# First MLP pipelined one tile deeper on VectorE and PE, recurrence operations bound behind the tile they are issued in, reciprocals of K in the second MLP

## The chip, the cores and the metric

The kernel runs on one core of a Trainium2 chip. The time is the device time of one execution in microseconds. The engines are called PE (TensorE, matrix products), DVE (VectorE), ACT (ScalarE), POOL (GpSimd) and SP (SyncE, which issues the DMAs). PE reads its left operand in a weight load (PEld) that overlaps the matmul before it.

## The reference

The reference is a gated linear recurrence over 768 steps for 32 heads, whose output goes through two MLPs. Cut to what matters:

```python
# recurrence, per batch and head (D = 48): a = a_re + i a_im, |a| clipped to 0.999
for t in range(S):
    S_re, S_im = ar * S_re - ai * S_im + k_t v_t^T, ar * S_im + ai * S_re
    y[t] = q_t @ S_re
# first MLP (384 -> 2048 -> 384)
h = x @ w_in
P = a[0] + a[1]*h + a[2]*h**2 + a[3]*h**3
Q = 1.0 + abs(b[0])*abs(h) + abs(b[1])*h**2
x = (P / (Q + 1e-06)) @ w_out
# second MLP (384 -> 1536 -> 384)
g = x @ w_gate
return (g * sigmoid(g) * (x @ w_val)) @ w_out2
```

All of it is float32. A product at float32 accuracy is made of products of a high and a low part (hi, lo) of each operand, three of the four.

## The kernel before

**Stages.** The 3072 tokens are worked off in six pairs of units, 512 tokens to a pair, numbered 0 to 5. The startup makes the recurrence inputs and attention of pair 0 and converts the first weights. Then each pair runs the first MLP (16 tiles of 128 hidden columns) and the second MLP (12 tiles), both in `moe`. PE's accumulators `acc` collect the output over the tiles of an MLP.

**A tile of the first MLP.** PE makes `ph` in nine up matmuls (L179 to L181). ACT makes `w` = |b1 ph| (L211) and `u` (L212, a scale and a bias). DVE forms numerator and denominator in three operations (L218 into `w`, L221 and L223 into `u`). ACT takes |w| (L222), then Ln and Exp into `r` (called at L223 to L225 of the code, recorded at L117, the line of the helper `fact`). The inner function `divide` puts on DVE `hi` (L228), `w` (L229) and `u` (L230), and on POOL `lo` (L231); it also queues the tile's nine down matmuls in `pend`, six with `hi` (L186, L187) and three with `lo` (L190). `flush` issues what is queued. `u` and `w` have three buffers each, `hi`, `lo` and `r` two. `HALF` is 1: in the iteration of tile f the code first flushes the down matmuls of tile f-2, then calls `divide` of tile f-1, then writes the three forming operations of tile f; an order dependence puts the first of them behind the last operation of `divide`.

**Between the MLPs** the output is split into `x1h` (ACT, L122) and `x1l` (DVE, L123).

**A tile of the second MLP.** PE makes `pg` and `pv` in 18 up matmuls; ACT takes silu of `pg` into `u` (L117); DVE multiplies by `pv` (`w`, called z in the code, L261); ACT rounds it to `hi` (L262); DVE makes `lo` (L265); nine down matmuls follow one tile later. The outputs are copied by ACT (L271) and stored.

**Work woven in.** While pair i runs, `tick`, called once in each tile, issues work of later pairs. First the recurrence's elementwise work of pair p = i + 1 and later: 36 steps a pair (`EW`): seeds, a scan of the complex gates, the products of Q (L531), and nine steps for K: squares (L566, L567), their reciprocals by Ln and Exp (recorded at L117 as `t`), two operations (L588, L589), and for each unit a scaling (L592) and products (L531). `ENDS` gives for each pair how far (in pairs) these steps are to be when its first and second MLP end, `SPAN` in how many tiles of the first MLP its share is issued. Second, the 17 attention steps of pair i + 1 on PE, ACT and DVE (`kT`, `pp`, `pm`, `S`, `py`, `xl`; L619 to L652); `AT` gives the tiles in which they are issued, `HOLD` how many are kept for the gap between the MLPs.

**Order.** The code is issued in program order; a scheduler then fills each engine's queue by priority, with its own estimates of when operands are ready, and so pulls operations that depend on nothing late ahead of those that do. On the chip each engine runs its queue in order. Ln and Exp share one table on ACT, silu has another; a switch is an ACT_TABLE_LOAD (L104). `order(later, earlier)` adds a dependence that fixes the order of two instructions.

In pair 0 weights are also converted from their stored form (`raw`, L129 to L141, on DVE and ACT) as they are first needed, and written back for the later pairs.

## Time and profile before

| | before |
|---|---|
| median of 3 runs | 1451.88 us (1448.75 to 1460.53) |
| the profiled execution | 1443.08 us |
| its span, first to last instruction | 1441.2 us |
| mean granted TensorE clock (1 = 2.4 GHz, 0.5 = 1.2 GHz) | 0.919 |
| PE busy | 1149.0 us (80%) |
| DVE busy | 987.0 us (68%) |
| ACT busy | 699.1 us (49%) |
| POOL busy | 127.3 us (9%) |
| chain of work that ended last, by engine | PE 50%, DVE 21%, ACT 17%, POOL 5%, DMA 4% |

The shares of busy time are averages over stages with different limits, so the table alone doesn't say what bounds the kernel: the stages do. PE's matmuls are pipelined and their ends are modelled, so PE's busy time also holds short waits. The profile names an instruction by its line, its engine, what it writes and what it reads (buffer numbers left out). An entry in brackets is the idle time of the engine just ahead of the instruction, with what ended it. "L12" is line 12 of the kernel.

### The profile page before, as it was taken

The page shows a single profiled execution, that of the slowest core. Times are in us where ns is not written, and L with a number is a line of the kernel's source. Part 1 is how long each engine was busy: PE and PEld are TensorE (multiplying, and loading weights), DVE is VectorE, ACT ScalarE, POOL GpSimd, SP SyncE. Part 2 cuts the span into 40 slices and gives each one's busy share as a digit, 9 for nine tenths or more (in the row PEclk, how much of TensorE's full clock was granted, in tenths as well). Part 3 has the DMA queues.
Part 4 walks back from the last instruction along what each step waited for, and adds up shares of the span by engine and source line. Part 5 has one row for each costly group of instructions (what it writes and reads, how often), then busy time and mean ns, then how long its engine had stood idle before and what let it go on. Part 6 is the DMA issues. An engine that isn't in the chain of part 4 may idle for free.

```text
span 1441.2 us, 15114 instructions
## 1 busy us (share of the span) xinstructions
PE 1149.0 (80%) x5314; PEld 916.1 (64%) x5314; DVE 987.0 (68%) x1601; ACT 699.1 (49%) x1081; POOL 127.3 (9%) x110
## 2 busy tenths in 40 slices
...
GB/s 227 110 232 206 175 252 246 191 187 224 204 248 245 250 138 130 231 239 227 115 112 136 282 225 161 115 100 201 274 195 146 116 151 195 180 109 131 132 175 47
DMA packets 128291, 261.51 MB, mean 181 GB/s; under 512 B 8016, under 2 KB 85072, under 8 KB 127440
## 3 DMA queue, kind: packets, MB, share of 16 engines
...
HBM read 210.11 MB, written 50.33 MB: 181 GB/s over the span
## 4 chain that ended last, share of the span: by engine, by line
PE 50%; DVE 21%; ACT 17%; POOL 5%; DMA 4%; issue 3%; POOLq 0%; SPq 0%; ACTq 0%; DVEq 0%
ACT r L117 5%; POOL lo L231 5%; PE acc L190 5%; PE acc L186 5%; PE acc L187 4%; PE pg L179 4%; PE pg L180 4%; PE pg L181 4%; PE pv L179 3%; PE pv L180 3%; PE pv L181 3%; PE py L646 3%; DVE hi L228 3%; DVE u L230 3%; ACT u L212 3%
## 5 line engine op out<-in xcount | busy, mean ns | idle before, releaser
L186 PE MATMUL acc<-hi,wt 128*128 128x512 f32 x504 | 220.6, 438 | 69.0 <-DVE hi L228 68.8
L231 POOL TENSOR_TENSOR lo<-u,r 128x512 fp32r<-128x512 f32 x96 | 126.6, 1319 | 1229.8 <-DVE u L230 1088.1
L187 PE MATMUL acc<-hi,wt 128*128 128x512 f32 x504 | 212.3, 421 | 0.0
L190 PE MATMUL acc<-lo,wt 128*128 128x512 f32 x504 | 159.2, 425 | 59.4 <-POOL lo L231 58.9
L261 DVE TENSOR_TENSOR w<-pv,u 128x512 f32<-128x512 f32 x72 | 49.8, 691 | 190.8 <-PE pv L181 190.7
L186 PEld LDWEIGHTS acc<-hi,wt 128*128 128x128 f32 x504 | 102.5, 203 | 114.6 <-DVE hi L228 93.2
L179 PE MATMUL ph<-xh,wt 128*128 128x512 f32 x288 | 124.4, 432 | 49.0 <-ACT wt L138 35.7
L190 PEld LDWEIGHTS acc<-lo,wt 128*128 128x128 f32 x504 | 93.0, 198 | 105.6 <-POOL lo L231 90.8
L211 ACT ACTIVATE w<-ph,par 128x512 f32<-128x512 f32 x96 | 65.9, 686 | 157.5 <-DVE u L230 132.5
L228 DVE SCALAR_TENSOR_TENSOR hi<-u,par,r 128x512 fp32r<-128x512 f32 x96 | 71.9, 749 | 92.9 <-ACT r L117 92.4
L181 PE MATMUL ph<-xh,wt 128*128 128x512 f32 x288 | 119.0, 413 | 2.9 <-DVE wt L141 2.9
L180 PE MATMUL ph<-xl,wt 128*128 128x512 f32 x288 | 118.8, 412 | 0.0
L117 ACT ACTIVATE u<-pg 128x512 f32<-128x512 f32 x72 | 43.0, 598 | 154.9 <-PE pg L181 154.9
L187 PEld LDWEIGHTS acc<-hi,wt 128*128 128x128 f32 x504 | 103.1, 205 | 19.5
L262 ACT ACTIVATE hi<-w 128x512 fp32r<-128x512 f32 x72 | 45.4, 630 | 124.8 <-DVE w L261 124.5
L179 PEld LDWEIGHTS ph<-xh,wt 128*128 128x128 f32 x288 | 58.2, 202 | 72.6 <-ACT wt L138 38.9
L619 PE MATMUL pk<-ident,st 96*128 96x96 f32 x160 | 23.8, 275 | 92.5 <-DMA st<-qs 91.8
L212 ACT ACTIVATE u<-ph,par 128x512 f32<-128x512 f32 x96 | 74.7, 778 | 40.7 <-POOL lo L231 40.5
L179 PE MATMUL pg<-x1h,wt 128*128 128x512 f32 x216 | 89.0, 412 | 1.1 <-ACT x1h L122 1.1
L180 PE MATMUL pg<-x1l,wt 128*128 128x512 f32 x216 | 86.7, 401 | 0.0
L181 PE MATMUL pg<-x1h,wt 128*128 128x512 f32 x216 | 86.4, 400 | 0.0
L179 PE MATMUL pv<-x1h,wt 128*128 128x512 f32 x216 | 85.0, 393 | 0.0
(110 smaller groups left out, 2513.0 us busy)
## 6 DMA issues: line engine op xcount, KB each, us to landing
...
```

Of the source, the lines that this page charges most:

```text
L117: i = act(*args, **kw)
L179: t_.matmul(ph, whi, xh[:, k, :], start=(k == 0), stop=False)
L180: t_.matmul(ph, whi, xl[:, k, :], start=False, stop=False)
L181: t_.matmul(ph, wlo, xh[:, k, :], start=False, stop=(k == KT - 1))
L186: t_.matmul(acc[m], wt[:, 0, c : c + 128], hi, start=st, stop=False)
L187: t_.matmul(acc[m], wt[:, 1, c : c + 128], hi, start=False, stop=False)
L190: t_.matmul(acc[m], wt[:, 0, c : c + 128], lo, start=False, stop=sp)
L211: act(w, ph, AF.Abs, scale=b1)
L212: act(u, ph, AF.Identity, scale=a3, bias=a2)
L228: stt(hi, u, a0, r, ADD, MUL)
L231: g_.tensor_tensor(lo, u, r, MUL)
L261: tt(z, pv, sg, MUL)
```

## The change

Three things change. First, in the first MLP `divide` of tile f-1 is called after the forming operations of tile f and after that tile's `tick`, its first operation is ordered behind the last forming operation of tile f, and the forming operations of tile f are ordered behind the last operation of the `divide` before. `flush(gf)` keeps one tile's down matmuls pending, so they are issued one tile later. `hi` and `lo` are allocated in `divide`. Second, DVE operations issued by `tick` through `tt` and `stt` get an order dependence: they stay behind the tile's last forming operation (first MLP) or behind its `z` (second MLP). All operations through `tt` and `stt` are then recorded at L87, the line of the wrapper. Third, the tables `ENDS`, `SPAN` and `AT` change: pair 1's to pair 3's second MLPs now finish a pair's 36 steps, K's reciprocals among them, where before eight steps were left for the next pair's first MLP, and the attention steps of pairs 2 to 5 begin at tile 1 instead of tile 4 (pair 1: 12 instead of 10).

```diff
@@ -48,9 +48,9 @@
 EARLY1 = range(7, 16)
 CV = (5, 4)
 EW = 36
-ENDS = ((1.06, 1.5), (2.06, 2.8), (3.06, 3.8), (4.06, 4.8), (5.0, 5.0), (5.0, 5.0))
-SPAN = (16, 10, 5, 5, 5, 5)
-AT = ((16, 16, 0, 11), (10, 16, 0, 6), (4, 16, 0, 1), (4, 16, 0, 1), (4, 16, 0, 1), (4, 16, 0, 1))
+ENDS = ((1.06, 1.5), (2.06, 3.0), (3.06, 4.0), (4.06, 5.0), (5.0, 5.0), (5.0, 5.0))
+SPAN = (16, 11, 8, 8, 5, 5)
+AT = ((16, 16, 0, 11), (12, 16, 0, 6), (1, 16, 0, 1), (1, 16, 0, 1), (1, 16, 0, 1), (1, 16, 0, 1))
 HOLD = (0, 3, 4, 4, 4, 0)
 XMAX = 1e18
 NTINY = 1e-30
@@ -77,7 +77,21 @@
 ):
     nc = tc.nc
     v_, s_, g_, t_ = nc.vector, nc.scalar, nc.gpsimd, nc.tensor
-    tt, stt, act = v_.tensor_tensor, v_.scalar_tensor_tensor, s_.activation
+    act = s_.activation
+    pin = {"on": False, "at": None}
+
+    def held_back(op):
+        def f(*args, **kw):
+            i = op(*args, **kw)
+            if pin["on"] and pin["at"] is not None:
+                order(i, pin["at"])
+            return i
+
+        return f
+
+    tt, stt = held_back(v_.tensor_tensor), held_back(v_.scalar_tensor_tensor)
     MUL, ADD, SUB, MIN, MAX = ALU.mult, ALU.add, ALU.subtract, ALU.min, ALU.max
 
     dram = ctx.enter_context(tc.tile_pool(name="dram", bufs=1, space=DRAM))
@@ -192,7 +206,7 @@
         def mt(tag, dt=F32):
             return mp.tile([128, gf, T], dt, tag=tag, name=tag, bufs=M_BUFS.get(tag, 3))
 
-        pend, half = [], []
+        pend, half, divided = [], [], []
 
         def flush(n):
             while len(pend) > n:
@@ -207,38 +221,36 @@
                 wts.append(wt)
                 up(ph[:, j, :], wt, 0, x_hi, x_lo)
             u, w, r = (mt(n) for n in ("u", "w", "r"))
-            hi, lo = mt("hi", F32R), mt("lo", F32R)
             act(w, ph, AF.Abs, scale=b1)
             act(u, ph, AF.Identity, scale=a3, bias=a2)
-            if len(half) > HALF - 1:
-                flush(0)
-                last = half.pop(0)()
-            else:
-                last = None
             p = stt(w, w, b0, ph, ADD, MUL)
-            if last is not None:
-                order(p, last)
+            if divided:
+                order(p, divided[-1])
             tt(u, u, ph, MUL)
             act(w, w, AF.Abs)
-            stt(u, u, a1, ph, ADD, MUL)
+            formed = stt(u, u, a1, ph, ADD, MUL)
             fact(r, w, AF.Ln, bias=cst[:, 2:3])
             fact(r, r, AF.Exp, scale=-1.0)
 
-            def divide(f=f, wts=wts, u=u, w=w, r=r, hi=hi, lo=lo):
-                stt(hi, u, a0, r, ADD, MUL)
+            def divide(f=f, wts=wts, u=u, w=w, r=r):
+                hi, lo = mt("hi", F32R), mt("lo", F32R)
+                first = stt(hi, u, a0, r, ADD, MUL)
                 stt(w, w, 1.0 + EPS, hi.bitcast(F32), ADD, MUL)
-                last = stt(u, u, a0, w, ADD, SUB)
+                divided.append(stt(u, u, a0, w, ADD, SUB))
                 g_.tensor_tensor(lo, u, r, MUL)
                 for j in range(gf):
                     pend.append((acc, wts[j], DM, hi[:, j, :], lo[:, j, :], f + j == 0, f + j == F1 - 1))
-                return last
+                return first
 
             half.append(divide)
-            tick(0)
+            tick(0, formed)
+            if len(half) > HALF:
+                flush(gf)
+                order(half.pop(0)(), formed)
         while half:
-            flush(0)
+            flush(gf)
             half.pop(0)()
-        tick(2)
+        tick(2, None)
         flush(0)
         xh = xp.tile([128, KT, T], F32R, tag="xh", name="x1h")
         xl = xp.tile([128, KT, T], F32R, tag="xl", name="x1l")
@@ -258,10 +270,10 @@
             sg, z = mt("u"), mt("w")
             hi, lo = mt("hi", F32R), mt("lo", F32R)
             fact(sg, pg, AF.Silu)
-            tt(z, pv, sg, MUL)
+            formed = tt(z, pv, sg, MUL)
             act(hi, z, AF.Copy)
             flush(0)
-            tick(1)
+            tick(1, formed)
             tt(lo, z, hi.bitcast(F32), SUB)
             for j in range(gf):
                 pend.append((acc2, wts[j], 0, hi[:, j, :], lo[:, j, :], f + j == 0, f + j == F2 - 1))
@@ -415,7 +427,7 @@
                         t_.transpose(px[:, m, :], rows[:, m * 128 : (m + 1) * 128], ident)
                     cs = slice(n * CH, (n + 1) * CH)
                     split(px, xh[:, :, cs], xl[:, :, cs])
-                moe(pools, 512, xh, xl, out[:, :, bass.ds(j * (UPB * 512) + k * 512, 512)], lambda ph: None, silu, feed(stored, pools[3]))
+                moe(pools, 512, xh, xl, out[:, :, bass.ds(j * (UPB * 512) + k * 512, 512)], lambda ph, ins: None, silu, feed(stored, pools[3]))
 
     with ExitStack() as es:
         ps = es.enter_context(tc.tile_pool(name="ps", bufs=5, space=PSUM))
@@ -749,10 +761,11 @@
                     next(at, None)
 
 
-            def tick(ph, cnt=[0, 0], eb=eb, e0=e0, e1=e1, n=n, at=at, at_to=at_to, at_n=at_n, w=AT[i], i=i):
+            def tick(ph, ins, cnt=[0, 0], eb=eb, e0=e0, e1=e1, n=n, at=at, at_to=at_to, at_n=at_n, w=AT[i], i=i):
                 if ph == 2:
                     at_to(at_done[0] + HOLD[i])
                     return
+                pin["on"], pin["at"] = True, ins
                 cnt[ph] += 1
                 t = cnt[ph]
                 lo, hi = ((eb, e0), (e0, e1))[ph]
@@ -764,6 +777,7 @@
                 if ph == 1 and t == n[1]:
                     ew_to(EW * (i + 1))
                     run(at)
+                pin["on"] = False
 
             if i:
                 lnexp()
```

What this does to the queues is shown at three places, from the lists of each engine's instructions in order. Numbers behind a name tell the buffers apart.

The first place is DVE in the first MLP of the last pair. `ph` is the output of the up matmuls; an operation that reads it belongs to the forming of a tile, one that writes or reads `hi` or reads `r` to the division. Before:

```order
L218 SCALAR_TENSOR_TENSOR w_8959<-w_8959,par_90,ph_8946 128x512
L221 TENSOR_TENSOR u_8958<-u_8958,ph_8946 128x512
L223 SCALAR_TENSOR_TENSOR u_8958<-u_8958,par_90,ph_8946 128x512
L228 SCALAR_TENSOR_TENSOR hi_8961<-u_8958,par_90,r_8960 128x512
L229 SCALAR_TENSOR_TENSOR w_8959<-w_8959,hi_8961 128x512
L230 SCALAR_TENSOR_TENSOR u_8958<-u_8958,par_90,w_8959 128x512
L218 SCALAR_TENSOR_TENSOR w_8997<-w_8997,par_90,ph_8984 128x512
L221 TENSOR_TENSOR u_8996<-u_8996,ph_8984 128x512
```

After, the same operations at L87:

```order
L87 SCALAR_TENSOR_TENSOR w_8916<-w_8916,par_90,ph_8903 128x512
L87 TENSOR_TENSOR u_8915<-u_8915,ph_8903 128x512
L87 SCALAR_TENSOR_TENSOR u_8915<-u_8915,par_90,ph_8903 128x512
L87 SCALAR_TENSOR_TENSOR hi_8935<-u_8877,par_90,r_8879 128x512
L87 SCALAR_TENSOR_TENSOR w_8878<-w_8878,hi_8935 128x512
L87 SCALAR_TENSOR_TENSOR u_8877<-u_8877,par_90,w_8878 128x512
L87 SCALAR_TENSOR_TENSOR w_8954<-w_8954,par_90,ph_8941 128x512
L87 TENSOR_TENSOR u_8953<-u_8953,ph_8941 128x512
L87 SCALAR_TENSOR_TENSOR u_8953<-u_8953,par_90,ph_8941 128x512
```

Before, a tile's division (`hi`, `w`, `u`) follows the forming of the same tile. Now the division of `u_8877` stands behind the forming of `u_8915`, the next tile.

The second place is DVE in the second MLP of pair 2: the tiles 2 to 4 of 12. `pv` is the value product of the second MLP; `qp` are the products of Q, `t6` squares of K. Before:

```order
L261 TENSOR_TENSOR w_5273<-pv_5249,u_5272 128x512
L531 TENSOR_TENSOR qp_5700<-q_5698,a_4421 128x8x6x16
L265 TENSOR_TENSOR lo_5275<-w_5273,hi_5274 128x512
L531 TENSOR_TENSOR qp_5700<-q_5698,a_4421 128x8x6x16
L531 TENSOR_TENSOR qp_5744<-q_5742,a_4421 128x8x6x16 x2
L567 TENSOR_TENSOR t6_5751<-t6_5751 128x8x96
L261 TENSOR_TENSOR w_5318<-pv_5294,u_5317 128x512
L567 TENSOR_TENSOR t6_5808<-t6_5808 128x8x96
L265 TENSOR_TENSOR lo_5320<-w_5318,hi_5319 128x512
L261 TENSOR_TENSOR w_5369<-pv_5345,u_5368 128x512
L265 TENSOR_TENSOR lo_5371<-w_5369,hi_5370 128x512
L261 TENSOR_TENSOR w_5416<-pv_5392,u_5415 128x512
```

After (`t3`, `a` and `T2` are the recurrence's scan):

```order
L87 TENSOR_TENSOR w_5277<-pv_5253,u_5276 128x512
L87 SCALAR_TENSOR_TENSOR t2_5244<-t1_4583,t2_5244 128x4x192
L87 TENSOR_TENSOR t3_5294<-a_4366 128x768
L87 TENSOR_TENSOR a_4366<-a_4366,t2_5244 128x1536
L87 TENSOR_TENSOR a_4366<-t3_5294 128x192 x2
L87 TENSOR_TENSOR lo_5279<-w_5277,hi_5278 128x512
L87 TENSOR_TENSOR t3_5294<-a_4366 128x768
L87 TENSOR_TENSOR w_5327<-pv_5303,u_5326 128x512
L87 TENSOR_TENSOR a_4366<-t3_5294 128x192 x2
L87 TENSOR_TENSOR t3_5294<-a_4366 128x768
L87 TENSOR_TENSOR lo_5329<-w_5327,hi_5328 128x512
L87 TENSOR_TENSOR a_4366<-t3_5294 128x192 x2
```

Before, the tiles' `w` and `lo` have at most three recurrence operations between them, and from the fourth tile on none; now scan operations of the next pair stand behind each `w`, some ahead of `lo` and some behind it.

The third place is ACT near the end of the same second MLP; `u` from `pg` is silu, `hi` the rounded product, `t6` K's squares and their Ln and Exp. After:

```order
L131 ACTIVATE u_5661<-pg_5637 128x512
L578 ACTIVATE t6_5679<-a_4366 128x1536
L578 ACTIVATE t6_5684<-a_4366 128x1536
L118 ACT_TABLE_LOAD
L274 ACTIVATE hi_5663<-w_5662 128x512
L131 ACTIVATE t6_5679<-t6_5679,cst_91 128x8x96
L131 ACTIVATE t6_5684<-t6_5684,cst_91 128x8x96
L131 ACTIVATE t6_5679<-t6_5679 128x8x96
L131 ACTIVATE t6_5684<-t6_5684 128x8x96
L118 ACT_TABLE_LOAD
L131 ACTIVATE u_5714<-pg_5694 128x512
L274 ACTIVATE hi_5716<-w_5715 128x512
```

Before, no table load stood between two tiles of a second MLP: the load and the Ln and Exp of K stood behind its last silu. Now K's squares, a load, the Ln and Exp and a load back stand between the silus of tiles 9 and 10 (counted from 0), and a third load stands behind the last silu for the next pair's first MLP.

## Rows read from the trace of the kernel before

**Rows 1.** Windows by stage: length, busy time per engine (instructions), PEclk, DMA share, GB/s.

```profile
0.00:168.50 168.50, 48.36 (x277) 45.61 (x277) 134.00 (x241) 75.12 (x107) 0.71 (x14) 0.85 0.57 189
168.50:308.40 139.90, 91.54 (x278) 60.87 (x279) 127.34 (x178) 100.51 (x152) 24.05 (x16) 0.77 0.66 222
308.40:427.00 118.60, 118.60 (x638) 101.92 (x638) 97.67 (x187) 68.15 (x123) 0.00 (x0) 0.90 0.62 211
427.00:557.70 130.70, 99.11 (x441) 74.81 (x439) 107.90 (x171) 77.06 (x116) 20.47 (x16) 0.91 0.63 205
557.70:644.60 86.90, 86.68 (x425) 72.44 (x424) 44.16 (x80) 26.90 (x42) 0.00 (x0) 1.00 0.70 214
644.60:777.60 133.00, 110.92 (x544) 89.20 (x542) 106.40 (x189) 75.18 (x120) 20.52 (x16) 0.90 0.46 148
777.60:854.60 77.00, 76.79 (x339) 62.98 (x338) 38.11 (x50) 24.93 (x37) 0.00 (x0) 1.00 0.77 236
854.60:982.90 128.30, 109.74 (x576) 88.43 (x575) 107.41 (x191) 74.81 (x117) 20.50 (x16) 0.92 0.43 139
982.90:1060.00 77.10, 76.88 (x339) 62.99 (x339) 39.64 (x57) 25.19 (x37) 0.00 (x0) 1.00 0.77 240
1060.00:1175.80 115.80, 100.94 (x528) 81.21 (x527) 79.55 (x116) 59.25 (x93) 20.53 (x16) 0.96 0.45 145
...
1252.60:1358.60 106.00, 78.58 (x279) 51.48 (x278) 67.26 (x96) 54.80 (x83) 20.52 (x16) 0.95 0.36 122
```

**Rows 2.** Timeline, first MLP of the last pair: start, duration, instruction [idle before, releaser].

```profile
1291.81 0.75 DVE L228 SCALAR_TENSOR_TENSOR hi<-u,par,r 128x512 fp32r<-128x512 f32 x1 [2.19 <-ACT r L117]
...
1293.33 0.75 DVE L230 SCALAR_TENSOR_TENSOR u<-u,par,w 128x512 f32<-128x512 f32 x1
...
1294.25 1.29 POOL L231 TENSOR_TENSOR lo<-u,r 128x512 fp32r<-128x512 f32 x1 [5.22 <-DVE u L230]
...
1295.57 0.78 ACT L212 ACTIVATE u<-ph,par 128x512 f32<-128x512 f32 x1 [0.71 <-POOL lo L231]
...
1296.24 0.62 ACT L222 ACTIVATE w<-w 128x512 f32<-128x512 f32 x1
...
1297.65 0.63 ACT L117 ACTIVATE r<-r 128x512 f32<-128x512 f32 x1
...
1298.32 0.75 DVE L228 SCALAR_TENSOR_TENSOR hi<-u,par,r 128x512 fp32r<-128x512 f32 x1 [2.20 <-ACT r L117]
```

**Rows 3.** Waits in the last pair's first MLP: total us, times, longest.

```profile
DVE hi L228 <- ACT r L117: 33.3, 16, 3.1
```

**Rows 4.** Timeline of ACT in the second MLP of pair 3.

```profile
1011.60 0.63 ACT L262 ACTIVATE hi<-w 128x512 fp32r<-128x512 f32 x1 [2.24 <-DVE w L261]
...
1017.72 0.63 ACT L262 ACTIVATE hi<-w 128x512 fp32r<-128x512 f32 x1 [2.24 <-DVE w L261]
```

**Rows 5.** Timeline of DVE in the first MLP of pair 3.

```profile
890.67 0.74 DVE L228 SCALAR_TENSOR_TENSOR hi<-u,par,r 128x512 fp32r<-128x512 f32 x1
...
895.32 1.89 DVE L469 TENSOR_TENSOR a<-a,t 128x1536 f32<-128x1536 f32 x1
...
898.66 0.74 DVE L228 SCALAR_TENSOR_TENSOR hi<-u,par,r 128x512 fp32r<-128x512 f32 x1
```

**Rows 6.** Groups by line, DVE, first and last of the recurrence's 36.

```profile
L437 DVE TENSOR_TENSOR t<-a 128x768 f32<-128x768 f32 x42 | 40.7, 969 | 0.4
...
L491 DVE MEMSET E<- 128x6 f32 x2 | 0.1, 63 | 0.0
```

**Rows 7.** Timeline of PE in the first MLP of pair 3, an attention step.

```profile
882.10 1.08 PE L623 MATMUL pp<-st 96*128 96x128 f32 x8
```

**Rows 8.** ACT, end of pair 1's second MLP (timeline), and its squares (by line).

```profile
636.76 1.28 ACT L104 ACT_TABLE_LOAD   x1
638.05 1.77 ACT L117 ACTIVATE t<-t,cst 128x768 f32<-128x768 f32 x2
...
L566 ACT ACTIVATE t<-a 128x1536 f32<-128x1536 f32 x12 | 17.5, 1478 | 0.2 <-DVE a L521 0.2
```

## The prediction

> **What bounds the kernel now.** I read the busy times by stage first [rows 1]: one window per MLP, cut where the first MLP's first ScalarE operation and the second MLP's first x1h start. In the last pair no attention and no recurrence work is left, and its first MLP still takes 106.0 us, with PE busy 78.6, DVE 67.3 and ACT 54.8: no engine is full. The timeline inside it shows why [rows 2]. From one `hi` to the next pass 6.51 us (1291.81 to 1298.32): DVE makes `hi`, `w`, `u` of tile k; GpSimd can then make `lo` (1294.25, 1.29 us); only when `lo` has released its `u` buffer does ACT write the `u` of a later tile (1295.57); behind that in ACT's queue stand |w|, Ln and Exp of tile k+1 (1296.24 to 1298.28); then DVE makes the next `hi`, after 2.20 us of idling. The waits of this stage say the same in sum: DVE waited 33.3 us for ACT's `r` in 16 tiles [rows 3]. It is a ring of dependences, run through once per tile. PE needs 18 matmuls a tile. In the second MLP, where PE never waits, ScalarE's `hi` comes every 6.12 us [rows 4] for 27 matmuls, 0.227 us each, so 18 are 4.1 us. DVE's six operations a tile are 67.3 us in 96 instructions [rows 1], 4.2 a tile; with small gaps I take 4.36.
>
> In pairs 1 to 3 the first MLP takes 130.7, 133.0 and 128.3 us [rows 1]. There recurrence work of a later pair stands between `hi`, `w` and `u`: one tile of pair 3 went from 890.67 to 898.66, 8.0 us, with a 1.89 us recurrence product inside it [rows 5]. The second MLPs of pairs 2 and 3 meanwhile have DVE busy for 38.1 and 39.6 of 77 us while PE is full at granted clock 1.00 [rows 1]: DVE is idle where PE is the bound, and loaded where the ring is.
>
> **The change, part by part.** *The ring.* In the new order (the first place shown) DVE forms tile k+1 before it divides tile k, and PE's down matmuls come one tile later. The ring then spans two tiles: 6.5/2 = 3.3 us a tile, and what is left is DVE's 4.36 and PE's 4.1. The `u` buffer that ACT waits for comes free by the same `lo`, now with a tile of DVE work to spare. Last pair: 106.0 less 15 steps of 6.51 leaves 8.4 us for filling and draining; 15 steps of 4.36, that 8.4, and 1.5 because the last two tiles' divisions now interleave make 75, so **-31**. If DVE and PE, so nearly equal, jostle at 4.7 a tile, it is -26.
>
> *The recurrence work in the first MLPs.* One pair's recurrence costs DVE 61.6 us: 36 groups of lines 162 to 168 and 437 to 592, from 40.7 us down, sum to 369.6 over six pairs [rows 6]. I priced each DVE row of both orders with the mean duration of its group. The first MLP's queue goes in pair 1 from 121.6 to 103.8 us, pair 2 from 123.3 to 81.8, pair 3 from 122.6 to 83.1, pair 4 from 84.2 to 79.8. PE has there 16 x 4.1 = 66 plus attention: 273 small matmuls a pair at about 0.1 us (eight took 1.08 [rows 7]), 13 of the 17 attention steps, so some 18 us: 84 in all. With 13 us more, the 8.4 of filling and draining and some 5 for waits of attention steps, I get 97 for pairs 2 to 4 against 133.0, 128.3 and 115.8: **-36, -31, -19**. Pair 1 is DVE's 103.8 plus 8: 112, **-19**. Attention could take back more: kT's copy stands in ACT's queue behind a `u` that waits for `lo`, so PE's attention matmuls can wait for `lo` and two ACT operations (1.29 + 0.78 + 0.62 = 2.7 us [rows 2]) four times a pair. The bounds are 0 and 11 us a pair; I take the 5, and keep the other 6 in each of three pairs, +18, for the range.
>
> *The second MLPs.* They take over what the first ones lose (the second place shown): pair 1's DVE queue goes from 41.8 to 78.9 us, pair 2's from 33.1 to 74.5, pair 3's from 36.0 to 75.5, against PE's 12 x 6.12 = 73.4. By tile pair 2 reads 4.8, 7.0, 6.8, 6.5, 6.9, 9.2, 6.0, 5.6, 5.9, 3.3, 6.2, 6.2: where DVE is above 6.1 it sets the step, in sum +6. That a tile costs the larger of the two and not their sum is shown by pair 0's second MLP: 97.7 us of DVE beside 118.6 of always busy PE at clock 0.90 [rows 1]; one after the other they would need over 73 + 98 = 171.
>
> *K's reciprocals* (the third place shown). Between two silus ACT now runs two squares, a table load, two Ln, two Exp and a second load. Before, the load and the Ln were at the end of the second MLP: load 1.28, two Ln 1.77, a square 1.48 [rows 8]. With two Exp taken as the Ln, the block is 2.96 + 1.28 + 1.77 + 1.77 + 1.28 = 9.1 us in a tile of 6.1; silu comes 3 us late, but its `down` stands behind the next tile's up matmuls (4.1 us). Bounds 0 and 3 a pair; I take 2.4. Second MLPs: **+3, +8.5, +7.5** (pair 1's was longer, 86.9, and absorbs more).
>
> The Trainium skill (page "ScalarE: Activation LUTs", section "What ACT_TABLE_LOAD costs") says that a switch costs 1283 ns for the load and about 1380 ns of drain. The trace has the first number exactly, but the first Ln started 1.29 us after the load did [rows 8], so no drain shows here. By the page the six added loads would cost up to 6 x 1.38 = 8 us more, by the row nothing.
>
> *Pair 0.* 43.6 us of pair 1's recurrence work used to run in the startup, where DVE was busy 134.0 of 168.5 us [rows 1]; bound behind a tile it moves into pair 0's first MLP, whose DVE queue goes from 141.7 to 167.5, and that stage already lasts as long as its queue (139.9, DVE 127.3 busy). That is +26. Against it the first conversions of weights find a freer DVE and the first up matmuls start about 10 us earlier by my walk through the order: **+16**, bounds 0 (the startup gives all of it back) and +26. Second MLP: 111.5 to 112.9, **+2**.
>
> Sum: +16 +2 -19 +3 -36 +8.5 -31 +7.5 -19 +0 -31 +0 = **-99 us**, made against the profiled execution of 1443.08 (span 1441.2): 1344. The median of the runs, 1451.88, lies 8.8 above it; with that the forecast is **1353 us**.
>
> **Rivals.** (a) *The pins cost much more.* DVE runs in order, and an operation bound behind a tile waits in line with everything behind it. In pair 0 conversions wait for their loads, and if those waits are no longer filled the stage costs +26 twice; that is +36 on top of the +16; with attention's +18 the gain is halved: -45, about 1407. For it: pair 0 has PEclk 0.77 [rows 1], the level of 1.2 GHz for some 46% of the stage, and PE waits there often. Against: pairs 4 and 5, with fewer recurrence rows, keep 0.95 and 0.96.
>
> (b) *The ring does not open*, because ACT still issues the waiting `u` ahead of |w|. Then the first MLPs keep their 6.5 us a tile; pairs 2 and 3 gain only what the moved work cost them above it (16 x 6.51 + 13 = 117: -16 and -11), and with the +37 of costs it ends at 1443 + 37 - 27 = 1453, by the median 1462. Against: the order puts a whole tile of DVE work between the `lo` and the first reader of that `u`.
>
> (c) *Slower.* Work bound behind `z` also stands ahead of `lo` of the same tile, and PE's down matmuls need `lo`. If PE could do nothing meanwhile, each second MLP of pairs 1 to 3 would take the 77 us of PE's pace and its 57 us of recurrence work one after the other, 134: +47, +57 and +57. With pair 0's +18 that is +179 against gains of 136: 1486 by the profiled run, 1495 by the median. It decides once 0.73 of that work is uncovered. Against: pair 0's second MLP [rows 1], where it is covered; the next tile's 18 up matmuls stand ahead of the waiting `down`.
>
> (d) *More than forecast*: the startup gives back all that pair 0 takes (+16 becomes 0), and attention fits into the tiles, so that pairs 2 to 4 need 84 + 8.4 = 92 instead of 97 (-15): 1322. For it: DVE was busy 0.8 of the startup. Against: PE and DVE then both have to run full.
>
> **Chances.** Forecast 0.60 (own range 1328 to 1380), (a) 0.20, (d) 0.08, (b) 0.05, (c) 0.07. The time is the forecast's. The range leaves out (b), (c), the part of (a) above 1412 and the far end of (d), together 0.2: 1315 to 1412. About 1% is what a measurement of this kernel can tell from no change: faster by more 0.87, within it 0.06 ((b) and a tail of (a)), slower 0.07 ((c)).
>
> **What would show it.** Ring right: `hi` to `hi` near 4.4 us in the last pair and no DVE wait for `r` of over 1 us; wrong: still 6.5. Moved work right: first MLPs of pairs 2 and 3 below 100 us, second ones at 84 to 86; (c) would show second MLPs above 110 with PE waiting for `lo`. Pair 0 right: its first MLP near 156; (a) would show it above 170, or PEclk below 0.85 in pairs 2 to 4. Reciprocals right: 18 loads of 1.28 us, the tile behind them late by under 3.5 us. The forecast is wrong if the second MLPs and pair 0 together give back over 80 us.

## The result and the profile after

The changed kernel takes 1341.18 us, the median of 4 runs (1337.3 to 1343.35), against 1455.05 (1448.75 to 1460.53, 4 runs) beside it: a ratio of 0.9216, 95% interval 0.9168 to 0.9263. The forecast was 1353 with a range of 1315 to 1412, and faster. The profiled execution has a span of 1339.4 us and a mean clock of 0.923; the sum of the forecast's terms, -99 us, meets -101.8 between the two spans.

| | after |
|---|---|
| span | 1339.4 us |
| PE busy | 1106.4 us (83%) |
| DVE busy | 984.0 us (73%) |
| ACT busy | 701.4 us (52%) |
| chain of work that ended last | PE 67%, DVE 16%, ACT 7%, POOL 1% |

The work is the same but for six more table loads on ACT; the chain moved to PE. These are the windows by stage, cut like [rows 1] (startup, then first and second MLP of each pair; columns: length, busy time of PE, weight loads, DVE, ACT and POOL with the number of instructions, PEclk, DMA share, GB/s):

```profile
0.00:156.80 156.80, 47.82 (x277) 45.62 (x277) 97.82 (x159) 61.92 (x89) 0.72 (x14) 0.88 0.60 203
156.80:321.40 164.60, 98.30 (x278) 65.30 (x279) 152.48 (x243) 105.04 (x157) 24.68 (x16) 0.72 0.53 174
321.40:434.60 113.20, 109.71 (x637) 93.43 (x636) 95.56 (x180) 74.40 (x134) 0.00 (x0) 1.00 0.73 251
434.60:545.20 110.60, 85.00 (x385) 66.21 (x385) 97.11 (x145) 75.27 (x112) 20.84 (x16) 0.92 0.70 225
545.20:638.90 93.70, 93.47 (x485) 78.84 (x485) 73.42 (x133) 33.28 (x48) 0.00 (x0) 1.00 0.61 198
638.90:739.60 100.70, 96.80 (x540) 83.90 (x539) 75.01 (x111) 70.41 (x118) 20.91 (x16) 0.93 0.62 201
739.60:817.70 78.10, 77.88 (x343) 63.45 (x342) 69.44 (x126) 30.82 (x43) 0.00 (x0) 1.00 0.70 226
817.70:929.20 111.50, 107.60 (x573) 94.02 (x571) 76.01 (x114) 70.78 (x116) 20.87 (x16) 0.86 0.54 167
929.20:1005.70 76.50, 76.26 (x336) 62.25 (x335) 68.92 (x131) 28.30 (x39) 0.00 (x0) 1.00 0.69 226
1005.70:1103.00 97.30, 94.44 (x531) 81.43 (x530) 74.99 (x111) 59.40 (x96) 20.88 (x16) 0.96 0.58 186
...
1179.80:1255.20 75.40, 68.01 (x278) 51.71 (x277) 65.66 (x96) 54.59 (x83) 20.96 (x16) 0.98 0.49 166
```

Stage by stage, against [rows 1]: the startup went from 168.5 to 156.8 us, pair 0's first MLP from 139.9 to 164.6, together +13.0. The first MLPs of pairs 1 to 5 went from 130.7, 133.0, 128.3, 115.8 and 106.0 to 110.6, 100.7, 111.5, 97.3 and 75.4. The second MLPs of pairs 2 and 3, into which the recurrence work moved (DVE busy 69.4 and 68.9 us where it was 38.1 and 39.6), take 78.1 and 76.5 us: +1.1 and -0.6.

The ring is open. This is the timeline of the last pair's first MLP, to be held against [rows 2] (start, duration, instruction, idle time ahead and what ended it):

```profile
1206.29 1.29 POOL L240 TENSOR_TENSOR lo<-u,r 128x512 fp32r<-128x512 f32 x1 [2.92 <-ACT r L131]
...
1207.41 0.75 DVE L87 SCALAR_TENSOR_TENSOR u<-u,par,ph 128x512 f32<-128x512 f32 x1
...
1207.61 0.78 ACT L225 ACTIVATE u<-ph,par 128x512 f32<-128x512 f32 x1 [0.71 <-POOL lo L240]
...
1208.08 0.75 DVE L87 SCALAR_TENSOR_TENSOR hi<-u,par,r 128x512 fp32r<-128x512 f32 x1
...
1208.29 0.62 ACT L230 ACTIVATE w<-w 128x512 f32<-128x512 f32 x1
...
1209.70 0.64 ACT L131 ACTIVATE r<-r 128x512 f32<-128x512 f32 x1
...
1212.29 0.75 DVE L87 SCALAR_TENSOR_TENSOR hi<-u,par,r 128x512 fp32r<-128x512 f32 x1
```

From `hi` to `hi` it is now 4.21 us (1208.08 to 1212.29) instead of 6.51. ACT's `u` (1207.61) still waits 0.71 us for `lo`, as before, and |w|, Ln and Exp still stand behind it. But DVE does not wait for them: at 1208.08 it starts the `hi` of the tile before, and when it comes to this tile's `hi` at 1212.29, its `r` has been there for two us (Exp ended at 1210.34, the sum of the row's start and duration). The waits of the stage:

```profile
ACT u L225 <- POOL lo L240: 9.0, 13, 0.7
DVE w L87 <- ACT u L225: 7.0, 2, 5.4
```

The wait of [rows 3], `hi` for `r`, is down from 33.3 us to 0.2, in one tile. ACT's wait for `lo` is still there, 13 times, but it costs no `hi` a wait of over 0.2 us. Most of what is left of DVE's idling is one start of 5.4 us.

### The profile page after: what moved, and what is told of

Read it like the earlier page. It is cut to its first block, busy times and chain, and to the rows that moved or that the text cites. A ratio compares the mean times of both kernels' runs of the same rounds, so it can differ in the third digit from the quotient of the medians.

```text
span 1339.4 us, 15191 instructions
## 1 busy us (share of the span) xinstructions
PE 1106.4 (83%) x5314; PEld 910.4 (68%) x5314; DVE 984.0 (73%) x1601; ACT 701.4 (52%) x1087; POOL 129.9 (10%) x110
## 4 chain that ended last, share of the span: by engine, by line
PE 67%; DVE 16%; ACT 7%; DMA 6%; issue 3%; POOL 1%; POOLq 0%; SPq 0%; ACTq 0%; DVEq 0%
PE acc L204 8%; PE acc L200 7%; PE acc L201 7%; PE pg L193 4%; PE pg L195 4%; PE py L658 4%; PE pg L194 4%; DVE t L87 4%; PE pv L193 4%; PE pv L194 4%; PE pv L195 4%; PE pp L635 4%; PE ph L193 3%; DMA wt<-w1s 3%; PE ph L194 3%; PE ph L195 3%
## 5 line engine op out<-in xcount | busy, mean ns | idle before, releaser
L200 PE MATMUL acc<-hi,wt 128*128 128x512 f32 x504 | 217.0, 431 | 40.9 <-DVE hi L87 40.9
L201 PE MATMUL acc<-hi,wt 128*128 128x512 f32 x504 | 210.6, 418 | 0.0
L204 PE MATMUL acc<-lo,wt 128*128 128x512 f32 x504 | 153.3, 412 | 27.7 <-POOL lo L240 27.6
L193 PE MATMUL ph<-xh,wt 128*128 128x512 f32 x288 | 122.0, 424 | 55.5 <-ACT wt L152 29.9
L87 DVE TENSOR_TENSOR w<-pv,u 128x512 f32<-128x512 f32 x72 | 49.7, 690 | 127.1 <-PE pv L195 113.0
L204 PEld LDWEIGHTS acc<-lo,wt 128*128 128x128 f32 x504 | 96.1, 196 | 57.8 <-POOL lo L240 37.6
L201 PEld LDWEIGHTS acc<-hi,wt 128*128 128x128 f32 x504 | 102.8, 204 | 19.5
L224 ACT ACTIVATE w<-ph,par 128x512 f32<-128x512 f32 x96 | 65.7, 684 | 87.8 <-DVE u L87 51.1
L193 PEld LDWEIGHTS ph<-xh,wt 128*128 128x128 f32 x288 | 57.8, 201 | 78.9 <-ACT wt L152 33.3
L131 ACT ACTIVATE u<-pg 128x512 f32<-128x512 f32 x72 | 43.0, 597 | 130.6 <-PE pg L195 130.6
L87 DVE SCALAR_TENSOR_TENSOR w<-w,par,ph 128x512 f32<-128x512 f32 x96 | 71.4, 744 | 38.9 <-ACT u L225 38.6
L193 PE MATMUL pg<-x1h,wt 128*128 128x512 f32 x216 | 85.9, 398 | 3.3 <-ACT wt L152 2.0
L631 PEld LDWEIGHTS pk<-ident,st 96*128 96x128 f32 x160 | 20.9, 167 | 95.4 <-issue 92.0
L195 PE MATMUL pg<-x1h,wt 128*128 128x512 f32 x216 | 84.3, 390 | 0.3 <-DVE wt L87 0.3
```

Of the source, the lines that this page charges most:

```text
L87: i = op(*args, **kw)
L193: t_.matmul(ph, whi, xh[:, k, :], start=(k == 0), stop=False)
L195: t_.matmul(ph, wlo, xh[:, k, :], start=False, stop=(k == KT - 1))
L200: t_.matmul(acc[m], wt[:, 0, c : c + 128], hi, start=st, stop=False)
L201: t_.matmul(acc[m], wt[:, 1, c : c + 128], hi, start=False, stop=False)
L204: t_.matmul(acc[m], wt[:, 0, c : c + 128], lo, start=False, stop=sp)
```

## The experiments

All ratios are against the kernel before on the same chip, with 95% intervals; two runs have one time only. The kernel before took between 1444.5 and 1455.1 us beside the different kernels, so times of different kernels are compared through the ratios or stage by stage. The table has the length of the stages, cut as above from each kernel's profiled execution: 0A is the first MLP of pair 0, 0B its second (us). 4B is left out; it is 76.8 to 77.1 us in all kernels but one (f2, 81.6). So is 5B with the end of the kernel, 82.6 to 85.2.

| kernel | time | ratio | start | 0A | 0B | 1A | 1B | 2A | 2B | 3A | 3B | 4A | 5A |
|---|---|---|---|---|---|---|---|---|---|---|---|---|---|
| before | 1455.1 | 1 | 168.5 | 139.9 | 118.6 | 130.6 | 86.9 | 133.0 | 77.1 | 128.3 | 77.1 | 115.8 | 105.9 |
| the change | 1341.2 | 0.9216 | 156.8 | 164.6 | 113.2 | 110.6 | 93.6 | 100.7 | 78.1 | 111.5 | 76.6 | 97.2 | 75.4 |
| e1: depth | 1336.1 | 0.9262 | 168.3 | 131.6 | 114.5 | 117.6 | 86.9 | 110.9 | 77.1 | 113.6 | 77.1 | 96.3 | 76.2 |
| f3: depth, tables | 1334.3 | 0.9235 | 168.3 | 131.9 | 114.5 | 111.3 | 93.2 | 106.9 | 77.5 | 117.0 | 77.2 | 93.6 | 74.5 |
| e3: depth, binding | 1383.7 | 0.9590 | 157.5 | 164.7 | 113.2 | 118.2 | 86.8 | 115.6 | 77.0 | 111.9 | 77.0 | 115.1 | 77.3 |
| e2: binding, tables | 1416.4 | 0.9831 | 157.3 | 165.9 | 119.0 | 120.4 | 93.7 | 109.0 | 78.1 | 114.5 | 77.1 | 111.3 | 106.9 |
| h1: binding | 1434.4 | 0.9924 | 157.0 | 166.8 | 117.0 | 127.4 | 88.4 | 118.3 | 78.1 | 121.4 | 77.4 | 111.6 | 107.1 |
| f1: change, pair 0 free | 1322.4 | 0.9149 | 168.5 | 129.4 | 111.5 | 113.2 | 95.3 | 100.7 | 78.1 | 107.0 | 76.6 | 98.2 | 75.9 |
| f2: change, HOLD 0 | 1364.8 | 0.9425 | 157.0 | 167.2 | 117.4 | 121.5 | 96.5 | 100.8 | 84.7 | 101.2 | 83.0 | 99.4 | 74.5 |
| f4: pair 0 free, HOLD 2 | 1315.2 | 0.9086 | 169.5 | 131.7 | 114.7 | 117.8 | 95.3 | 95.8 | 78.1 | 104.1 | 76.6 | 97.4 | 76.7 |
| g1: pair 0 free, HOLD 3, 2 | 1309.9 | 0.9032 | 169.0 | 130.6 | 111.6 | 112.7 | 95.3 | 95.8 | 78.1 | 106.4 | 76.5 | 100.3 | 74.7 |
| h2: pairs 0, 1 free, HOLD 3, 2 | 1313.0 | 0.9067 | 169.4 | 130.9 | 111.3 | 119.7 | 94.4 | 92.9 | 78.1 | 106.4 | 76.6 | 100.3 | 76.3 |
| e4: before, 4 u | 1408.5 | one time | 168.4 | 139.4 | 117.1 | 124.1 | 86.9 | 124.5 | 77.1 | 126.6 | 77.1 | 110.1 | 95.7 |
| g2: before, 4 u and w | 1415.1 | one time | 176.8 | 139.9 | 111.1 | 125.3 | 87.0 | 121.5 | 77.2 | 126.6 | 77.2 | 108.1 | 103.2 |

### Which part of the change gives the gain

The theory was that the deeper order opens the ring. The rival was that in pairs 1 to 3 it is the binding and moving of the recurrence work that helps. The change has three parts (depth, binding, tables), so they were taken apart. The depth alone:

```diff
... (ENDS, SPAN, AT as in the kernel before)
-                pin["on"], pin["at"] = True, ins
+                pin["on"], pin["at"] = False, ins
```

> The changed kernel with the old tables and with no operation bound behind a tile: the deeper order of the first MLP alone. Theory 1 (the ring was the bound, and the scheduler itself then leaves less recurrence work between hi, w and u): DVE's queue in the first MLPs goes from 119, 121, 120 us (pairs 1 to 3, order priced with row durations) to 107, 106, 106; with 8 to 12 us of filling the stages take 115 to 118, pairs 4 and 5 take 97 and 75 as in the changed kernel: in sum about -100 us, 1345 to 1360. Theory 2 (binding and moving the work is what helps pairs 1 to 3): only pairs 4 and 5 gain, -50, and pairs 1 to 3 -5 each: about 1390.

Measured: 1336.1 us (1333.45 to 1340.88), ratio 0.9262, interval 0.9228 to 0.9296. That is the whole gain as far as the runs can tell: the interval overlaps the change's. Its startup, pair 0's first MLP and pair 2's first MLP:

```profile
0.00:168.30 168.30, 46.53 (x277) 43.91 (x277) 133.83 (x241) 75.02 (x106) 0.72 (x14) 0.86 0.56 189
168.30:299.90 131.60, 88.95 (x278) 62.91 (x279) 124.86 (x169) 97.70 (x148) 25.46 (x16) 0.77 0.70 231
618.90:729.80 110.90, 98.71 (x544) 81.69 (x543) 97.82 (x142) 73.78 (x119) 21.75 (x16) 0.94 0.55 173
```

Pair 0 pays nothing (startup and first MLP end at 299.9; after the full change at 321.4, before at 308.4), and pairs 1 to 3 still gain 13.0, 22.1 and 14.7 us with unbound work: the binding is not needed for it. The moving is not excluded by this run. DVE ran 142 instructions in pair 2's first MLP where it ran 189 before [rows 1] and 111 in the changed kernel, and was busy for 97.8 us instead of 106.4; the second MLPs of pairs 2 and 3 took it up (DVE busy 47.9 and 49.1 us, where it was 38.1 and 39.6). So in the deeper order the scheduler itself moved some 9 us of recurrence work out of each of these first MLPs. How much of the gain of pairs 1 to 3 is this moving and how much the ring, no run tells apart; in pairs 4 and 5 DVE's work hardly changed (77.9 and 65.7 us busy, before 79.6 and 67.3), and they gain 19.5 and 29.7.

The binding and the tables, at the old depth (the changed kernel with the first MLP's old code):

```diff
+            if len(half) > HALF - 1:
+                flush(0)
+                last = half.pop(0)()
...
             p = stt(w, w, b0, ph, ADD, MUL)
-            if divided:
-                order(p, divided[-1])
+            if last is not None:
+                order(p, last)
...
             tick(0, formed)
-            if len(half) > HALF:
-                flush(gf)
-                order(half.pop(0)(), formed)
```

> The opposite: the old order of forming and dividing in the first MLP (division of a tile right behind its forming, down matmuls two tiles later), with the bound recurrence work and the new tables. Theory 1: the ring of 6.5 us a tile stays, so pairs 2 and 3 take 16 x 6.5 + 13 = 117 instead of 133 and 128, pair 4 stays at 115 and pair 5 at 106, and pair 0 with the startup costs 13 more: about 1435. Theory 2: pairs 1 to 3 gain as much as in the changed kernel (-20, -32, -17), less pair 0's 13: about 1400.

Measured: 1416.4 us, ratio 0.9831 (0.9782 to 0.9880), between the two expectations. The last pair's step stays at 6.5 us (106.9 us); pairs 1 to 3 gain 10.2, 24.0 and 13.8, more than the 6.5 us a tile that I had taken as a floor: there are steps of 5.0 to 5.8 us in pairs 2 to 4. The trace shows where they come from. Number an MLP's tiles from 0. In the last pair ACT runs `u` of tile 5 ahead of |w| of tile 3, and it waited for `lo` 13 times (9.1 us); in pair 2 it runs `u` of tile 4 there, whose buffer came free a tile earlier, and it waited for `lo` once (0.7 us). So in pairs 1 to 3 the binding and the tables alone take off about as much as the depth alone (10.2, 24.0 and 13.8 against 13.0, 22.1 and 14.7), and the two overlap: together they take 20.1, 32.3 and 16.8. The rival holds there in part. It falls for the kernel as a whole, because pairs 4 and 5 gain only 4.5 and -1.0 without the depth, and pair 0 pays 14.8.

The binding with the depth but without the tables:

```diff
... (ENDS, SPAN, AT as in the kernel before)
```

> The changed kernel with the old tables ENDS, SPAN and AT: K's reciprocals back in the first MLP of the next pair, 12 instead of 18 table loads. If moving them pays by DVE's queue (first MLPs of pairs 2 to 4 at 90, 91, 88 us instead of 80, 81, 78), this is 5 to 10 us a pair slower: 1355 to 1370. If the extra loads and the block on ScalarE cost the second MLPs what I reckoned (2.4 a pair) and the first MLPs are bound by PE anyway, it is 3 to 8 us faster: 1333 to 1338.

Measured: 1383.7 us, ratio 0.9590 (0.9559 to 0.9621), a loss of 42.5 us against the change by the medians (34.2 between the profiled executions) and more than either expectation. Bound behind a tile, K's last steps come where they are issued, in the next pair's first MLP, and attention waits for them. This is the first attention matmul of pair 4's first MLP (PE, timeline), in this kernel 33.9 us after the MLP's start at 1021.8:

```profile
1055.70 0.87 PE L631 MATMUL pk<-ident,st 96*128 96x96 f32 x4 [1.38 <-DMA st<-qs]
```

In the changed kernel it comes 11.1 us after the start at 1005.7:

```profile
1016.82 0.49 PE L631 MATMUL pk<-ident,st 96*128 96x96 f32 x4
```

A part of this distance is the tables' own: in e1, with the same old tables and nothing bound, it comes 21.5 us after the start. The rest is the binding: K's last products end 28.7 us after the start here and 11.1 in e1. Attention then has to fit into what is left: pair 4's first MLP takes 115.1 us instead of 97.2, pair 2's 115.6 instead of 100.7. In e1 the two take 96.3 and 110.9. So the tables' part is needed by the binding. Without binding it does nothing that the runs can tell:

```diff
-                pin["on"], pin["at"] = True, ins
+                pin["on"], pin["at"] = False, ins
```

> The deeper order with the new tables and with no operation bound: against the deeper order alone (1336.1) it shows what the tables do without the binding. If the tables only matter because bound operations come too late otherwise (1383.7 with binding and old tables), this is within 6 us of 1336. If moving K's reciprocals saves VectorE's queue by itself, the first MLPs of pairs 2 to 4 lose 3 to 4 us each: 1322 to 1328; if its six table loads cost by themselves, 1340 to 1345.

Measured: 1334.3 us, ratio 0.9235 (0.9169 to 0.9301) against 0.9262 for the depth alone. Last, the binding alone, at the old depth with the old tables (the kernel of e2, and):

```diff
... (ENDS, SPAN, AT as in the kernel before)
```

> The kernel before with the binding alone: old order of forming and dividing, old tables. With the deeper order the binding without the new tables was 3% slower than with them, and attention's first matmul in pair 4 waited for K's products. If that is the binding's own price, it shows here too: against the binding with the new tables (1416) some 30 to 45 us more, 1440 to 1460, no better than before. If it needs the deeper order, 1415 to 1425.

Measured: 1434.4 us, ratio 0.9924 (0.9887 to 0.9960), between the expectations: 18 us worse than with the tables by the medians and 13 by the ratios, not 30 to 45. The price of late K's is there at either depth (pair 2's first MLP 118.3 against 109.0, pair 3's 121.4 against 114.5). Pair 4's is the same in both (111.6 and 111.3), though attention starts 37.7 us into it here and 11.8 in e2: at the old depth the stage is as long without the delay.

### The ring, by its buffers

If ACT's wait for `lo` closes the ring, a fourth buffer of `u` should shorten the step without touching the order.

```diff
-M_BUFS = {"hi": 2, "lo": 2, "r": 2}
+M_BUFS = {"hi": 2, "lo": 2, "r": 2, "u": 4}
-            ysb = atp.tile([128, DM], F32, tag="ysb", name="ysb")
+            ysb = atp.tile([128, DM], F32, tag="ysb", name="ysb", bufs=1)
```

> The kernel before with a fourth buffer of u (and one buffer of ysb instead of two, to make room): the order is not touched, only ScalarE's wait for lo is taken away. If that wait closes the ring, the step from hi to hi in the last pair falls from 6.5 to about 5.1 us, because |w|, Ln and Exp start 1.3 us earlier: last first MLP 106 to 85, pair 4's from 116 to 100, in all 1405 to 1420. If the order on VectorE alone (dividing a tile right behind its forming) makes the 6.5 us, nothing changes: 6.5 us and 1450.

Measured: 1408.45 us, one time, in the range; but the step is 5.69 us and not 5.1, and the last first MLP 95.7. Timeline of this kernel, last pair:

```profile
1275.02 0.75 DVE L228 SCALAR_TENSOR_TENSOR hi<-u,par,r 128x512 fp32r<-128x512 f32 x1 [1.38 <-ACT r L117]
...
1277.38 0.69 ACT L211 ACTIVATE w<-ph,par 128x512 f32<-128x512 f32 x1 [2.39 <-DVE u L230]
...
1277.97 0.77 ACT L212 ACTIVATE u<-ph,par 128x512 f32<-128x512 f32 x1
...
1280.71 0.75 DVE L228 SCALAR_TENSOR_TENSOR hi<-u,par,r 128x512 fp32r<-128x512 f32 x1 [1.38 <-ACT r L117]
```

`u` (1277.97) no longer waits, but the `w` ahead of it (1277.38) starts only when DVE has read the oldest `w`: a second dependence of the same kind. It was there before as well (ACT's `w` waited for DVE's `u` for 30.4 us, 13 times, in the last pair's first MLP), so what the fourth `u` removed is only the 0.71 us that `u` waited beyond it [rows 2]; the step fell by 0.82. So a fourth `w` as well:

```diff
-M_BUFS = {"hi": 2, "lo": 2, "r": 2}
+M_BUFS = {"hi": 2, "lo": 2, "r": 2, "u": 4, "w": 4}
-                pm = held[hh] = atp.tile([128, 4, CH], F32, tag="pm", name="pm", bufs=3)
+                pm = held[hh] = atp.tile([128, 4, CH], F32, tag="pm", name="pm", bufs=2)
```

> The kernel before with four buffers of u and of w (ysb 1 and pm 2 buffers instead of 2 and 3 to make room), order untouched. With the fourth u alone the step in the last pair was 5.7 us, and ScalarE's w then waited for VectorE's u. If that second wait closes the ring now, the step falls to about 5.1 (forming 2.9 us, then |w|, Ln, Exp 2.1), the last first MLP to 87 us, and the kernel to 1385 to 1400. If something else closes it, 5.7 and 1408.

Measured: 1415.11 us, one time, and a step of 6.50: a miss. Timeline:

```profile
1285.13 0.75 DVE L228 SCALAR_TENSOR_TENSOR hi<-u,par,r 128x512 fp32r<-128x512 f32 x1 [2.20 <-ACT r L117]
...
1287.49 0.69 ACT L211 ACTIVATE w<-ph,par 128x512 f32<-128x512 f32 x1 [2.39 <-DVE u L230]
...
1288.88 0.78 ACT L212 ACTIVATE u<-ph,par 128x512 f32<-128x512 f32 x1 [0.70 <-POOL lo L231]
...
1289.56 0.62 ACT L222 ACTIVATE w<-w 128x512 f32<-128x512 f32 x1
...
1291.63 0.75 DVE L228 SCALAR_TENSOR_TENSOR hi<-u,par,r 128x512 fp32r<-128x512 f32 x1 [2.20 <-ACT r L117]
```

`u` waits for `lo` again. The reason is in ACT's order. With the last pair's tiles numbered from 0, the kernel before and the one with four `u` have w7, u7 between |w|4 and |w|5; this one has them between |w|3 and |w|4. With one more buffer of both, the scheduler pulled the first operations of a tile one tile further ahead, where the oldest buffer is not free, and put |w| of the urgent tile behind them again. The changed kernel, with three buffers, has them between |w|5 and |w|6: its u7 waits for the `lo` of tile 4 on the way to the `hi` of tile 6, two tiles on, where before it stood on the way to the `hi` of tile 5. What closes the ring is that early operations of a far tile stand in ACT's queue ahead of the late ones of a near tile; more buffers let them stand earlier still.

### What pair 0 pays, and the tail of the first MLPs

```diff
-                pin["on"], pin["at"] = True, ins
+                pin["on"], pin["at"] = i > 0, ins
```

> The changed kernel, but the recurrence operations issued while pair 0 runs are not bound behind their tile (pairs 1 to 4 as in the change). If binding them is what pair 0 pays for (startup and first MLP took 321.4 us in the changed kernel, 299.9 with the deeper order alone), this ends some 20 us below the changed kernel: 1315 to 1325, with startup and first MLP near 300. If the conversions and their loads set that stage, it stays at 321 and 1341.

Measured: 1322.4 us, ratio 0.9149 (0.9086 to 0.9212), as expected: startup and first MLP end at 297.9. The binding costs pair 0 some 23 us, in which the startup's gain of 11.7 is already counted; this rests on the stages, for the ratio's interval overlaps that of the change. It lies apart from that of the depth alone (0.9228 to 0.9296): with pair 0 left out of it, binding and tables together do add about one per cent. The binding has a part in that: the four times here, 1317.77 to 1325.92 us, lie below the four of f3 in the same set, 1328.83 to 1339.33.

The other open point was the tail of pairs 2 and 3: after the last `hi` of the changed kernel the first MLP still takes 19.9 and 25.0 us. Windows on the stretches in it (columns as above):

```profile
907.00:928.00 21.00, 21.00 (x96) 19.84 (x96) 3.24 (x6) 1.96 (x4) 2.82 (x2) 0.52 0.15 50
723.00:734.00 11.00, 11.00 (x55) 10.44 (x55) 2.73 (x5) 1.47 (x3) 2.31 (x2) 0.53 0.15 51
```

PE is busy throughout, at a clock of 0.52 and 0.53. Pair 3's stretch in the timeline of PE (attention's `py`, two matmuls to a row, then the last down matmuls):

```profile
906.14 0.39 PE L658 MATMUL py<-v,pm 128*128 128x48 f32 x2
906.36 0.39 PE L657 MATMUL py<-S,st 96*128 96x48 f32 x2
...
908.95 0.63 PE L658 MATMUL py<-v,pm 128*128 128x48 f32 x2
909.38 0.63 PE L657 MATMUL py<-S,st 96*128 96x48 f32 x2
...
926.58 0.63 PE L200 MATMUL acc<-hi,wt 128*128 128x512 f32 x1
927.01 0.63 PE L201 MATMUL acc<-hi,wt 128*128 128x512 f32 x1
...
928.26 0.40 PE L200 MATMUL acc<-hi,wt 128*128 128x512 f32 x1
928.49 0.40 PE L201 MATMUL acc<-hi,wt 128*128 128x512 f32 x1
```

From the start of the row at 906.14 to that of the next it is 0.22 us, and from 908.95 0.43; from the 128x512 matmul at 926.58 to the next it is 0.43 too, and from 928.26 0.23 again. These are the attention steps that `HOLD` keeps for the gap, and the down matmuls behind them. So they were spread over the tiles:

```diff
-HOLD = (0, 3, 4, 4, 4, 0)
+HOLD = (0, 0, 0, 0, 0, 0)
```

> The changed kernel with HOLD at 0 for all pairs: no attention steps are kept for the gap between the MLPs, they are spread over the tiles of the first MLP instead. Theory A: after the last hi of pairs 2 and 3 the first MLP still took 19.9 and 25.0 us because the held attention matmuls of 48 columns run in a block in which the granted clock is 0.5 (11 and 21 us); spread out, the stages take about 95 instead of 100.7 and 111.5: 1318 to 1328. Theory B: PE has the same work either way and those stages are PE's sum: within 5 us of 1341.

Measured: 1364.8 us, ratio 0.9425 (0.9361 to 0.9490): 23.6 us worse by the medians, 29.9 between the profiled executions. Pair 3's first MLP did fall by 10.3 us to 101.2, with a clock of 0.95 instead of 0.86; but it also ran 525 matmul records instead of 573, so the fall can't be put to the clock alone. Pair 2's stayed at 100.8. The largest loss is pair 1's first MLP, 121.5 us instead of 110.6, whose cause was not followed up. And attention work slid into the second MLPs, pair 2's for example:

```profile
760.50:845.20 84.70, 83.80 (x391) 68.52 (x391) 70.67 (x128) 31.16 (x44) 0.00 (x0) 0.99 0.64 204
```

PE is busy for 83.8 of 84.7 us there, and 391 matmul records instead of the 343 above cost their full time: 84.7 us against 78.1; pair 3's second MLP became 6.4 us longer, pair 4's 4.8. Keeping two steps instead of four or none, with pair 0 free:

```diff
-HOLD = (0, 3, 4, 4, 4, 0)
+HOLD = (0, 2, 2, 2, 2, 0)
-                pin["on"], pin["at"] = True, ins
+                pin["on"], pin["at"] = i > 0, ins
```

> Both of the first two kernels of this set in part: nothing bound while pair 0 runs, and HOLD at 2 for pairs 1 to 4. If both effects are real and add: 1305 to 1318. If only the first is: 1315 to 1325. If neither, 1341.

Measured: 1315.2 us, ratio 0.9086 (0.9026 to 0.9147). That is the end of the first range and the start of the second, and the interval overlaps that of f1, so the total doesn't decide. By the stages pair 2's first MLP takes 95.8 and pair 3's 104.1 (f1: 100.7 and 107.0), but pair 1's 117.8 (f1: 113.2). With HOLD 3 in pair 1:

```diff
-HOLD = (0, 3, 4, 4, 4, 0)
+HOLD = (0, 3, 2, 2, 2, 0)
-                pin["on"], pin["at"] = True, ins
+                pin["on"], pin["at"] = i > 0, ins
```

> Nothing bound while pair 0 runs, HOLD 3 for pair 1 as in the change and 2 for pairs 2 to 4. Pair 1's first MLP took 113.2 us with HOLD 3 and 117.8 with HOLD 2, pairs 2 and 3 100.7 and 107.0 with HOLD 4 and 95.8 and 104.1 with HOLD 2. If these add, 1308 to 1315, below both kernels; if they don't (what pair 1 leaves, pair 2 takes), 1315 to 1325.

Measured: 1309.9 us (1302.93 to 1316.35, 6 runs), ratio 0.9032 (0.8998 to 0.9065). The interval lies below f1's and overlaps f4's. Only pair 2 keeps its gain from `HOLD`: pair 3's first MLP takes 106.4 us, 107.0 in f1, and pair 4's 100.3 instead of 98.2. This is the window of pair 2's first MLP in it, at a clock of 0.98 instead of 0.93:

```profile
619.20:714.90 95.70, 91.80 (x540) 79.18 (x539) 75.09 (x111) 71.22 (x117) 20.89 (x16) 0.98 0.66 212
```

And with pair 1 unbound as well:

```diff
-                pin["on"], pin["at"] = i > 0, ins
+                pin["on"], pin["at"] = i > 1, ins
```

> The deeper order and the new tables, bound only from pair 2 on, HOLD 3 for pair 1 and 2 for pairs 2 to 4. Pair 1's two MLPs took 208.0 us bound (the kernel of the set before) and 204.5 unbound in the kernel with the depth alone. If that 3.5 us holds, 1303 to 1310; if pair 2 then inherits later products, 1310 to 1318.

Measured: 1313.0 us, ratio 0.9067 (0.9017 to 0.9117); pair 1's two MLPs take 214.1 us, not 204.5. The time lies in the second range, but not for its reason: pair 2's first MLP got shorter (92.9 against 95.8), and pair 1 itself lost. The kernel can't be told from the one above.

## Why the prediction was right, point by point

**The ring.** Right in its mechanism and its size: 75.4 us in the last pair against 75 expected, step 4.21 against 4.36. Two small errors cancel in it: the 15 steps took 59.9 us instead of 65.4 (the last one 0.94), filling and draining 15.5 instead of 9.9. The buffer runs show that the wait for `lo` was one closing of the ring, and the missed one shows that it is ACT's order, not the number of buffers, that closes it. Rival (b) is excluded by the step, though what it rested on is still there: ACT does issue the waiting `u` ahead of a |w|, but of a tile whose division comes one tile later.

**The recurrence work in the first MLPs.** The sizes came out for pairs 1, 2 and 4 (-20.1, -32.3, -18.5 against -19, -36, -19) and not for pair 3 (-16.8 against -31). The step that failed there is "13 us for filling and draining": it took 25.0 us from the last `hi` alone, 21 of them at half the clock. Pair 2, with 11 us at half the clock, took 100.7. Some of pair 3's miss differs from one execution to the next: f1, with the same code in that stage, took 20.1 us there and 107.0 in all. PE's attention was reckoned too low as well: 273 matmuls at 0.1 us for 13 of 17 steps are 21 us and not 18, and the window ends behind the four steps that `HOLD` keeps, so nearly all of them run in it, some 27. The sign that the prediction named for these stages, below 100 us in pairs 2 and 3, was not met. And the reason that it gave for these terms was half wrong: it put them down to the queue that the moving shortens. The depth alone takes 13.0, 22.1, 14.7 and 19.5 us off pairs 1 to 4; binding and tables on top of it add 7.0, 10.2, 2.1 and take back 0.9, though in pairs 1 to 3 they take about as much as the depth where they stand alone (e2).

**The second MLPs.** The mechanism, the larger of PE and DVE and not the sum, held against rival (c): 78.1 and 76.5 us. The size did not: +8.5 and +7.5 expected, +1.1 and -0.6 measured, and the sign of 84 to 86 us was not met. Two things were mis-sized. DVE's queue was priced with full durations, 74.5 us, but neighbours overlap a little, and the windows show 69.4. And the excess of single tiles was added as if none could be caught up: pair 2's steps from z to z were 6.4, 7.4, 5.2, 6.3 around the heaviest one. Pair 1's cost +6.7 instead of +3: its second MLP also does the attention that its table puts there, 485 PE records where there were 425. Without any binding (f3) it takes as long, 93.2 us, so this is the tables' price, which the prediction left out; pair 1's first MLP is 6.3 us shorter for it (111.3 in f3, 117.6 in e1). Pair 0's was expected 2 us longer and came out 5.4 shorter: nearly the same number of matmul records ran at a granted clock of 1.00 where it had been 0.90 [rows 1], and the forecast had no term for the clock. That was luck.

**K's reciprocals.** Between two silus of pair 2 ACT ran the block that was reckoned at 9.1 us:

```profile
796.09 0.60 ACT L131 ACTIVATE u<-pg 128x512 f32<-128x512 f32 x1 [1.84 <-PE pg L195]
796.58 2.86 ACT L578 ACTIVATE t<-a 128x1536 f32<-128x1536 f32 x2
799.46 1.28 ACT L118 ACT_TABLE_LOAD   x1
800.75 0.63 ACT L274 ACTIVATE hi<-w 128x512 fp32r<-128x512 f32 x1
801.29 1.75 ACT L131 ACTIVATE t<-t,cst 128x768 f32<-128x768 f32 x2
802.94 1.56 ACT L131 ACTIVATE t<-t 128x768 f32<-128x768 f32 x2
804.52 1.28 ACT L118 ACT_TABLE_LOAD   x1
805.82 0.60 ACT L131 ACTIVATE u<-pg 128x512 f32<-128x512 f32 x1
```

From silu to silu it is 9.73 us, and `z` waited for it (DVE; start, duration, idle time):

```profile
799.30 0.69 DVE L87 TENSOR_TENSOR w<-pv,u 128x512 f32<-128x512 f32 x1
...
806.45 0.69 DVE L87 TENSOR_TENSOR w<-pv,u 128x512 f32<-128x512 f32 x1 [4.11 <-ACT u L131]
...
811.99 0.69 DVE L87 TENSOR_TENSOR w<-pv,u 128x512 f32<-128x512 f32 x1
```

DVE idled 4.11 us for it; the step is 7.15 us and the next one 5.54: together 12.7 against 12.2 for two steps of 6.1. The cost is half a microsecond, near the lower bound of 0 to 3, and not 2.4. The page "ScalarE: Activation LUTs" of the Trainium skill (section "What ACT_TABLE_LOAD costs") would have 1.38 us of drain with each load; here too the next ACTIVATE started 1.29 and 1.30 us after the load did (800.75 and 805.82), so none shows, and a sum by the page would have been further off.

**Pair 0.** +13.0 for startup and first MLP together against +16: right. The sign named for it, a first MLP near 156 us, was not met as it stands: it took 164.6, and the 10 us that the first up matmuls were to start earlier show as a startup that is 11.7 us shorter. f1 shows that it is the binding: without it, 23 us less. Rival (a), which had pair 0's first MLP above 170 us, did not come. Its other sign, a PEclk below 0.85 in pairs 2 to 4, came near in pair 3 alone (0.86). A cost of its kind, by another path, is real in e3, where bound work came too late for attention and the ratio lost 3.7 points.

**The sum** was right to 3 us partly because errors cancelled: pair 3's first MLP gave 14 us less than expected, the second MLPs of pairs 0, 2 and 3 some 23 us more, pairs 1 and 2 took back 6. And it did not ask what the depth would do alone; by the runs, the binding and the tables together, as the change has them, add nothing to it that can be told (0.9216 against 0.9262, intervals overlapping): the stages show that what they save in pairs 1 to 3 is paid in pair 0 and in pair 1's second MLP.
